# Nyström attention with a two-layer network: attention steps give way while TensorE's program block is on its way

## The chip, the cores and the metric

One core of one Trainium2 chip runs the kernel. The metric is device time of one execution in microseconds (us). The kernel before took 282.48 us, the median of three runs (282.12 to 282.77).

## The reference

Eight batches of eight heads, 576 positions, head dimension 64, all float32 in and out. Attention goes over 32 landmarks, each the mean of 18 neighbouring positions. Its output is the input of a normalised two-layer network with a residual.

```python
q_lm = q.reshape(B, H, m, S // m, D).mean(axis=3)      # m = 32
k_lm = k.reshape(B, H, m, S // m, D).mean(axis=3)
A  = sm(q, k_lm)                                       # sm: softmax of scaled products
Bm = sm(q_lm, k_lm)
C  = sm(q_lm, k)
Z = Bm.transpose(0, 1, 3, 2) / (norm1(Bm) * norminf(Bm) + 1e-06)
for _ in range(6):
    Z = 2 * Z - Z @ Bm @ Z
x = (A @ Z @ C @ v)                                    # then heads side by side: 8 x 576 x 512
xn = (x - mean(x)) / sqrt(var(x) + 1e-06) * g_ln
out = x + np.maximum(xn @ w_ch1, 0.0) @ w_ch2          # 512 -> 2048 -> 512
```

## The kernel before

All matmuls are fp16 with fp32 sums. Nothing in the kernel leaves the order of instructions to a scheduler: every instruction that `keep` records stays at its place in its engine's queue. The order is made while the program is built, by a planner inside the kernel.

**Four streams.** `run()` holds four generators. `attentions()` (number 0) makes the attention of the batches, in sets: batch 1, batch 2, batches 3 and 4, batches 5 and 6, batch 7 (batch 0 is done before `run()`). `first_layers()` (1) makes the hidden layer, batch by batch: 16 chunks of 128 hidden units, each four matmuls into a tile `psh`, then a relu into `hT`. `rows0[0]` (2) makes the attention rows of batch 0. `second_layers()` (3) makes the second layer from `hT` and `w2_16`, 16 matmuls with 512 columns for each block of 128 rows; batches 4 to 7 use seven products of half blocks instead of eight (the tiles `w2mix`).

**A step.** Each generator yields a function that says from which time on its next step could run without waiting, by the planner's own estimates. `run()` asks all four, takes the first in the order 0, 1, 2, 3 whose time has come, and lets it emit its instructions. So attention goes ahead of all else, and the second layer, which is always one matmul, fills what is left. If none is ready, the earliest is taken, or small matmuls on zeros (`warm`) are put in. `help_out()` gives VectorE, GpSimd and SyncE their side jobs in between: loads, casts (`nat`, `natv`), transposes (`xT`), landmark sums (`part`, `asum`), statistics, stores.

**The clock of the planner.** `Clock` keeps an estimate of when each engine is free and when each tile was written. It also counts matmuls. TensorE's program reaches the engine in blocks, and `Clock` assumes that a block holds `BLOCK` = 127 matmuls, that the first ends at matmul 116 (`mark`), and that the next one's fetch takes 5000 ns from the mark on while loads are running, 3300 ns otherwise (`fetched`). `calm(n)` returns `fetched` if n more matmuls would reach the mark, and 0 otherwise; once batch 3 is in its second layer (`late()`), 20 matmuls are added.

```python
def calm(self, n):

    return self.fetched if self.count + n + (20 if late() else 0) >= self.mark else 0.0
```

**Attention of a set** (`attention2`), in TensorE's order: landmark products and scores of the landmarks with k (`psec`), the gram product, then six iterations (`iterate`: 8 or 16 small matmuls into `bank`, then one update of `st` on VectorE), and between them, from `side_work`: the scores of q (`psea`), the product with v (`pscv`, 72 matmuls in two parts or one), and for each half batch `divisors`: two matmuls into `psd`, a logarithm and an exponential on ScalarE into `lns`, a product into `ea` on GpSimd. Then `pszt` and `pszc` (16 or 32 small matmuls), the copy `zt`, the products `zcbd` on VectorE, and at last the rows of the set (`rows_of`: two to four matmuls from `ea` and `zcbd` for each block of rows, then a copy into `xblk`). `psec`, `psea`, `pscv`, `psd`, `pszt`, `pszc` and the first layer's `psh` share two PSUM buffers; four banks serve the rest.

In the kernel before, `calm` is part of the time of three kinds of steps alone: the landmark and k scores (64 matmuls), the q scores (64), and the parts of the product with v.

**The first layer** of batch b+1 can begin when its attention is `ready` and the second layer is at batch b. Its `product_of_heads` makes 8 matmuls from `zt` and `w1_16` into two banks, which are cast to `m16`; `chunk` takes `m16` and `ea` to `psh`. While a first layer runs, the second layer can still do the batch before, as long as that has work left.

Of the kernel before, what the change touches and what calls it, by code (L numbers as in the profile page):

```python
# [20 lines left out]
def kernel(  # L21
# [196 lines left out]
    clock = Clock()  # L218
# [6 lines left out]
    class Ring:  # L225
# [16 lines left out]
        def next(self, tag, k=1):  # L242
            ring = self.rings.get(tag)
            if ring is None or len(ring) - 1 + k <= ring[0]:
                return 0.0
            olds = ring[1:len(ring) + k - ring[0]]
            if any(o in self.pinned for o in olds):
                return NEVER
            return clock.WAY + max(max(clock.wrote.get(o, (0.0,))[0], clock.used.get(o, (0.0,))[0])
                                   for o in olds)  # L250
# [215 lines left out]
    def warm(n, cols):  # L466
        idle = banks.take([P, 512])
        for _ in range(n):
            MM(idle[:, 0:cols], zeros[:, 0:P], zeros[:, 0:cols])
# [1014 lines left out]
    def attentions():  # L1484
        for c in sets:
            for y in range(len(c.units) // 2):
                yield lambda: c.spread_ready(y)
                c.spread(y)
            yield from attention2(c.bs, c)

    def first_layers():
        for b in range(B):
            yield lambda: 0.0 if b == 0 or (b in ready and current[0] == b - 1
                                            and (b <= LAST_WHOLE or len(centered) == 4)) else NEVER
            yield from first_layer(b)
            first_done.add(b)
            if b >= FAST:
                h_left.extend((b, i, k) for i in range(3) for k in (0, 4))
            if b == 0:
                keep_tail(0)  # L1500
# [3 lines left out]
    def second_layers():  # L1504
        for b in range(B):
            yield lambda: 0.0 if b in first_done else NEVER
            current[0] = b
            if b:
                keep_tail(b)
            yield from second_layer(b)  # L1510

    def run():
        streams = [attentions(), first_layers(), rows0[0], second_layers()]
        waits = [next(g) for g in streams]
        while any(waits):
            help_out()
            now = clock.now() + 60
            at = [w() if w else 2 * NEVER for w in waits]
            k = next((k for k in range(4) if at[k] <= now), None)
            if k is None:  # L1520
                k = at.index(min(at))
                if at[k] >= NEVER:
                    clock.free["PE"] = clock.now() + 200
                    stuck[0] += 1
                    assert stuck[0] < 2000, (at, current)
                    continue
                if at[k] > now + 250 and clock.share() < 0.5 and banks.next() <= now:
                    warm(1, 256)
                    continue
            waits[k] = next(streams[k], None)  # L1530
# [45 lines left out]
    next(a0)  # L1576
    next(a0)
    run()
    help_out(True)

# [29 lines left out]
```

## Time and profile before

| what | number |
|---|---|
| median of 3 runs | 282.48 us |
| the profiled execution | 282.81 us |
| its span, first to last instruction | 281.0 us |
| VectorE busy | 212.3 us (76%) |
| ScalarE busy | 161.9 us (58%) |
| mean granted TensorE clock | 0.997 |
| second layer, `bank<-w,hT`, 528 matmuls | 109.2 us busy |
| first layer, `psh<-ea,m`, 512 matmuls | 76.9 us busy |
| relu on ScalarE, `hT<-psh`, 115 | 71.0 us busy, 652 ns each |
| HBM read and written | 36.70 MB, 9.44 MB |

Times in a timeline are us from the span's start; a row is a run of like instructions, with start, length, engine, line, what is written and read, the count, and in brackets how long the engine stood idle before and what ended that. Matmuls overlap, so the length of one (0.38 us for a 512-column one) is more than its share of a run. All matmuls have the line of the helper that records them; they are told apart by their tiles. "issue" is a wait for nothing that the profile shows.

### The profile page before, as it was taken

The numbers are of one execution on the slowest core, as the hardware profiler recorded it, in microseconds if no ns is written. First come the engines' busy times: TensorE is split into PE (matmuls) and PEld (weight loads), VectorE is DVE, ScalarE is ACT, GpSimd is POOL, SyncE is SP. The second block draws the span as 40 slices with busy tenths as digits, with TensorE's granted clock in tenths as the row PEclk, the third lists the DMA queues.
The fourth block names the chain that finished last, engine by engine and source line by source line (L and its number), as shares of the span: only waits on it lengthen the run. The fifth ranks groups of instructions, "written<-read, shape, count | busy, mean of one in ns | idle before, by whom it ended". The sixth has DMA issues, their size and how long they took to land.

```text
span 281.0 us, 8678 instructions
## 1 busy us (share of the span) xinstructions
PE 266.2 (95%) x3618; PEld 165.6 (59%) x3618; DVE 212.3 (76%) x479; ACT 161.9 (58%) x287; POOL 160.1 (57%) x187
## 2 busy tenths in 40 slices
PE   7988999999999999889989999999999999999994
PEld 7744554355444564344555645567877666678883
DVE  3558985999999847888978384697885499748761
ACT  2676954368554887148889754698248733671000
POOL 5368778999999999978999999310000040100000
PEclk9999999999999999999999999999999999999998
DMA  7999999989745579893750101310060005300606
GB/s 244 384 387 388 388 388 392 354 278 266 246 126 160 152 249 304 265 279 95 221 188 2 34 8 45 72 40 0 2 144 9 1 5 118 72 0 2 149 22 167
DMA packets 23375, 46.70 MB, mean 166 GB/s; under 512 B 2212, under 2 KB 2472, under 8 KB 23336
## 3 DMA queue, kind: packets, MB, share of 16 engines
q1 hardware_dynamic: 23176, 46.02, 51.9%
q8 instruction: 28, 0.46, 0.7%
q10 hardware_dynamic: 160, 0.13, 0.2%
q14 instruction: 11, 0.09, 0.1%
HBM read 36.70 MB, written 9.44 MB: 164 GB/s over the span
## 4 chain that ended last, share of the span: by engine, by line
PE 79%; DVE 9%; ACT 5%; issue 3%; DMA 2%; SPq 0%; DVEq 0%; ACTq 0%
PE bank L274 51%; PE psh L274 21%; DMA stg<-in_q_dram 2%; ACT hT L268 2%; DVE xblk L268 2%; PE pscv L274 2%; DVE m L268 2%; DVE xT L268 1%; PE psec L274 1%; PE psd L274 1%; DVE part L268 1%; ACT ec L268 1%; DVE hT L268 1%; ACT lns L268 1%; PE psea L274 1%
## 5 line engine op out<-in xcount | busy, mean ns | idle before, releaser
L274 PE MATMUL bank<-w,hT 128*128 128x512 f16 (+1 forms) x528 | 109.2, 335 | 1.1 <-issue 1.0
L268 ACT ACTIVATE hT<-psh 128x576 f16<-128x576 f32 x115 | 71.0, 652 | 17.4 <-PE psh L274 16.0
L274 PE MATMUL psh<-ea,m 128*128 128x288 f16 x512 | 76.9, 286 | 2.8 <-ACT hT L268 2.1
L274 PEld LDWEIGHTS <-hT 128*128 128x128 f16 x656 | 60.4, 98 | 32.2 <-issue 6.9
L274 PEld LDWEIGHTS <-m 128*128 128x128 f16 x512 | 47.9, 97 | 25.3 <-issue 10.1
L268 DVE SCALAR_TENSOR_TENSOR xblk<-bank,rstd,xblk 128x256 f32<-128x256 f32 (+1 forms) x77 | 39.2, 541 | 18.2 <-PE bank L274 18.2
L268 POOL TENSOR_TENSOR ea<-ea,lns 128x576 f16<-128x576 f16 x14 | 18.1, 1306 | 47.2 <-ACT lns L268 47.0
L268 POOL CAST nat<-stg 128x1152 f16<-128x1152 f32 x28 | 32.6, 1181 | 2.0 <-DMA stg<-in_k_dram 1.1
L268 POOL CAST natv<-stg 64x1152 f16<-64x1152 f32 (+1 forms) x23 | 26.7, 1161 | 8.8 <-DMA stg<-in_v_dram 7.9
L268 ACT COPY xblk<-bank 128x512 f32<-128x512 f32 (+1 forms) x34 | 19.1, 588 | 12.2 <-PE bank L274 12.0
L268 DVE BATCH_NORM_STATS2 six<-xblk 128x6 f32<-128x512 f32 x36 | 24.2, 671 | 0.0
L268 ACT CAST m<-bank 128x512 f16<-128x512 f32 x30 | 17.0, 588 | 9.9 <-PE bank L274 9.9
L268 DVE STREAM_TRANSPOSE xT<-nat 128x576 uint32<-128x576 uint32 x28 | 21.4, 765 | 0.6 <-POOL nat L268 0.6
L268 ACT ACTIVATE lns<-psd 128x576 f32<-128x576 f32 x16 | 10.3, 646 | 17.8 <-PE psd L274 16.7
L268 DVE TENSOR_REDUCE part<-xT 128x32 f16<-128x576 f16 x28 | 20.0, 742 | 0.2
L268 POOL TENSOR_TENSOR asum<-asum 128x256 f32<-128x256 f32 (+1 forms) x28 | 18.0, 644 | 2.2
L268 DVE CAST m<-bank 128x512 f16<-128x512 f32 x18 | 12.2, 679 | 7.3 <-PE bank L274 7.2
L268 POOL TENSOR_TENSOR asum<-nat 128x512 f32<-128x512 f16 x14 | 16.5, 1178 | 1.1
L274 PE MATMUL bank<-w2mix,hT 128*128 128x256 f16 x128 | 16.5, 273 | 0.0
L274 PE MATMUL bank<-w2mix 128*128 128x256 f16 x128 | 16.0, 273 | 0.0
L268 DVE SCALAR_TENSOR_TENSOR st<-st,bank 128x128 f16<-128x128 f16 (+2 forms) x36 | 11.1, 308 | 6.4 <-PE bank L274 6.0
L274 PE MATMUL bank<-zcbd,ea 128*128 128x256 f16 (+1 forms) x80 | 14.4, 275 | 1.0 <-DVE m L268 0.8
(123 smaller groups left out, 341.6 us busy)
## 6 DMA issues: line engine op xcount, KB each, us to landing
stg<-in_q_dram SPq DMA_DIRECT2D x16, 576.0 KB, 5.7
stg<-in_k_dram SPq DMA_DIRECT2D x16, 576.0 KB, 5.4
stg<-in_v_dram SPq DMA_DIRECT2D x16, 576.0 KB, 7.1
out_dram<-xblk SPq DMA_DIRECT2D x70, 128.0 KB, 2.3
wstg<-in_moe_w_ch_dram SPq DMA_DIRECT2D x16, 512.0 KB, 7.1
out_dram<-xblk ACTq DMA_DIRECT2D x2, 64.0 KB, 2.3
out_dram<-xblk SPq DMA_DIRECT2D x2, 64.0 KB, 2.1
g_rows<-in_moe_g_ln_dram SPq DMA_DIRECT2D x1, 2.0 KB
```

What stands on the lines that cost most here:

```text
L268: return lambda *args, **kw: keep(getattr(self.engine, op)(*args, **kw))
L274: keep(nc.tensor.matmul(o, l, r, start=start, stop=stop, tile_position=(rb, cb), skip_group_check=(skip or cb != 0)))
```

## The change

The time of every step of stream 0 is raised to `calm(16)`. When 16 more matmuls (36 once batch 3 is in its second layer) would reach the planner's mark, no step of attention counts as ready before the estimated end of the fetch, whatever its own time was; the other streams' steps are taken in the meantime if they are ready. No instruction and no wait is put into the program by this line; only the order in which the planner emits steps, and what follows from it (which engine takes a copy, which side job comes when, how many warm matmuls are put in), can differ.

```diff
@@ -1516,6 +1516,8 @@
             help_out()
             now = clock.now() + 60
             at = [w() if w else 2 * NEVER for w in waits]
+            if waits[0]:
+                at[0] = max(at[0], clock.calm(16))
             k = next((k for k in range(4) if at[k] <= now), None)
             if k is None:
                 k = at.index(min(at))
```

## The prediction

> **What bounds the kernel.** I read the whole page first, then the chain of waits from 108 to 130 us, the stretches table, and last the timelines of TensorE and ScalarE from 119 to 147 us.
>
> ```profile
> span 281.0 us, 8678 instructions
> PE 266.2 (95%) x3618; PEld 165.6 (59%) x3618; DVE 212.3 (76%) x479; ACT 161.9 (58%) x287; POOL 160.1 (57%) x187
> q8 instruction: 28, 0.46, 0.7%
> ```
>
> TensorE sets the time: 266.2 of 281.0 us. Its program comes as 28 transfers of 16 KB. 0.46 MB over 7236 weight loads and matmuls is 64 bytes each, so one transfer holds 128 matmuls with their loads. Below, a matmul has its number in TensorE's order, from 0.
>
> ```profile
> 113.99 1.20 issue
> ...
> 119.25 0.49 issue
> ...
> 123.03 0.99 issue
> ```
>
> These three pieces of the chain are TensorE idle with nothing to wait for. They stand before matmuls 1503, 1631 and 1759, which are 128 apart: the ends of blocks. In the trace the transfers for them end at 113.58, 118.39 and 122.65, and the matmuls start 1.35 to 1.6 us later. Together 2.68 us; no other block end shows a gap of this kind. So 2.68 us is all that better timing of blocks can win.
>
> ```profile
> core 0: us, PE busy (x) PEld busy (x) DVE busy (x) ACT busy (x) POOL busy (x), PEclk, DMA share, GB/s
> 108.00:113.00 5.00, 5.00 (x120) 2.37 (x108) 4.82 (x14) 2.94 (x5) 4.68 (x7) 1.00 0.98 326
> 119.00:124.00 5.00, 3.54 (x130) 1.97 (x130) 3.93 (x12) 2.67 (x4) 4.68 (x6) 1.00 0.94 275
> ```
>
> Why there: the DMA engines are 0.98 and 0.94 busy, so the transfer for matmul 1503 starts only at 112.70, and the blocks are short of large matmuls. Matmuls 1631 to 1758 hold 72 of pscv and 47 of the iteration, but 5 of the second layer (0.216 us each: 11 of them from 172.36 to 174.73).
>
> [...]
>
> **The change, part by part.** It adds no instruction that waits. The planner only takes another stream's step while calm(16) says that the mark is near. By the two programs' orders attention stands back at five places: matmuls 612, 1631, 1754, 2374 and 2511. Added work: two warm matmuls (0.1 us each). Two relus and two casts of m16 go from ScalarE to VectorE, one row copy and one zt copy the other way.
>
> *Stalls at 1503 and 1631: kept.* The planner's marks are 116+127k (1513, 1640, 1767), the trace's ends 9, 9 and 8 matmuls sooner. Matmuls 1375 to 1502 hold 16 second-layer products in both programs, 1503 to 1630 hold 11 in both. So 1.20 and 0.49 stay: 0. Bounds -1.2 to +1.2, as loads that fall otherwise could free or delay a fetch.
>
> *Stall at 1759: removed.* At 1631 second-layer matmuls now stand first: the block holds 20 instead of 5. From rows: 119.74, 7 of them (1.51), 16 iteration products (0.22, 119.74 to 119.96), pscv (0.69), two psd (0.35), 2 second-layer (0.43), iteration 0.22, 2 (0.43), psd 0.35: 123.94. Matmul 1759 is the tenth of the next 12: 125.88, after the 124.02 at which its block was usable. Gain 0.99.
>
> *What pays for it: the chain to the next batch's first layer.* The 12 end at 126.53, the last iteration at 126.75; then both remaining psd pairs start (before: 125.31 for the last-but-one).
>
> ```profile
> 125.31 0.41 PE L274 MATMUL psd<-ea,bones 128*128 128x288 f16 x2
> 127.83 0.30 PE L274 MATMUL pszt<-st,cv 32*64 32x32 f16 x16
> 128.07 0.25 PE L274 MATMUL pszc<-cv,st 32*32 32x64 f16 x16
> 128.79 0.41 PE L274 MATMUL bank<-w,zt 64*32 64x512 f16 x8
> 130.88 0.65 PE L274 MATMUL psh<-ea,m 128*128 128x288 f16 x4
> 146.18 0.60 PE L274 MATMUL bank<-w,hT 128*128 128x512 f16 x2
> ```
>
> ```profile
> 125.81 0.65 ACT L268 ACTIVATE lns<-psd 128x576 f32<-128x576 f32 x1 [1.91 <-PE psd L274]
> 126.50 0.68 ACT L268 ACTIVATE lns<-lns 128x576 f32<-128x576 f32 x1
> 127.09 0.63 ACT L268 ACTIVATE lns<-psd 128x576 f32<-128x576 f32 x1
> 127.75 0.68 ACT L268 ACTIVATE lns<-lns 128x576 f32<-128x576 f32 x1
> 128.34 0.35 ACT L268 CAST zt<-pszt 128x256 f16<-128x256 f32 x1
> 129.26 1.07 ACT L268 CAST m<-bank 128x512 f16<-128x512 f32 x2 [0.57 <-PE bank L274]
> ```
>
> ScalarE works in order: the copy zt stands behind four passes over lns, so the eight products with zt start 3.48 us after the psd pair (125.31 to 128.79). Before, eleven second-layer matmuls (2.38), two psd pairs and 32 small products (0.42) filled these 3.48 us. Now only four (0.86), the pairs (0.59) and the 32 are left: 1.6 us of new idle time. 126.75+3.48 = 130.23 against 128.79: the chain is 1.44 late, with the gain of 0.99 already in it. Behind it the six second-layer matmuls that stood among the row products are used up too: 28 after 1631 before, 27 now, none after zt. TensorE has no filler until 146.18.
>
> How much of 1.44 lasts to 146.18 is settled by ScalarE, which paces the 16 chunks. From the start of zt (128.34) to the phase's last relu (ends 146.59) it spans 18.25 us, of which 2.30 idle (0.57, 0.21, 0.68, 0.19, 0.26, 0.20, 0.19 in its timeline): 15.95 of work. Changed: one relu fewer (0.60 pitch), one copy more (0.55): 15.9, from 126.75+3.03 = 129.78. With no idle it ends at 145.7 (0.9 early), with all of it at 148.0 (1.4 late). The first chunks now stand between the row products, so ScalarE has copies queued where it waited 0.21 and 0.68; the wait for m stays. That leaves about 1.5 idle: 147.2. Value +0.6, bounds -0.9 and +1.4.
>
> Cover that this needs: on POOL a nat cast with its sums (1.15+1.16+1.26+0.43 = 4.0) now stands ahead of the last two ea products. These end at about 133.35 instead of 129.8; the row products that read them come at about 134.9. Were that cover gone, they would be late by the difference, at most 1.
>
> *Place 612.* Before z, 20 second-layer matmuls instead of 18 from 600 on. The iterations queue behind two xblk updates on VectorE (1.41), so pszt starts at about 53.3 instead of 52.60, with 0.43 of work done ahead. The first chunk is then 1.0 late, since two reductions (1.34) stand ahead of the zcbd products. But VectorE, which is busy without a break from 53.06 to 62.32 and there ends the wait for m, has 9.26 us from zsum to the second m before and about 7.5 after (a transpose, three reductions and a row copy now stand ahead of it or on ScalarE, one w1 update of 0.87 comes in). From about 54.6 that is 62.1. 0, bounds -0.2 and +0.5. One k load goes ahead of stores in SP's queue, one pair of stores past another: SP stands idle on waits between them, 0.
>
> *Places 2374 and 2511.* TensorE has no idle gap over 0.2 us there and second-layer work remains until the first layer; the pairs of psd also stand together, but nine second-layer matmuls (1.94) cover the ScalarE chain. One iteration waits for its st behind cv on VectorE: +0.1, bounds -0.1 and +0.4. Place 1078, where only the order shifts: 0. From matmul 2900 on the orders agree.
>
> **Sum.** 0.6+0.1 = +0.7 us. Span 281.0 to 281.7. The profiled execution took 282.81 around its span; the median of the runs is 282.48, and 283.2 is against that. 0.2% (0.57 us) is what can be told from no change.
>
> **Rivals.**
> 1. *ScalarE absorbs it* (faster). If the 2.30 us of idle time give way as the chunks come earlier, the phase ends up to 0.9 sooner: about 281.6. For: so much idle time, fewer row copies in a lump. Against: it begins 1.44 later and psum buffers are two. Decides when over 1.44 of the idle time vanishes; under 281.9 when 1.9 does. Chance 0.19.
> 2. *The whole delay lasts*, or a fetch stall comes back elsewhere: 1.4 to 2.4 late, 283.9 to 284.9. For: no filler is left, and 1.60 us of idle are certain once ScalarE's order stands. Against: idle 0.89 falls away. 0.22.
> 3. *The change misses its aim and nothing shows*: gain and delay cancel, 282.5. Two of three stalls stay as the marks don't meet the trace's ends. 0.11.
>
> **Numbers.** Likeliest, partial recovery: 0.48, own range 282.8 to 283.9; of it 0.08 lies within 0.2%. So slower 0.40+0.22 = 0.62, same 0.08+0.11 = 0.19, faster 0.19. The range to leave about one in ten on either side: 281.5 to 284.5, which also takes in most of the fetch bound.
>
> **What would show it.** In the changed profile: issue gaps near 1.2 and 0.5 us before the psea products and in second-layer matmuls at 1631, none before 1759; TensorE idle some 1.6 us in all before and after pszc; zt some 3.4 us after the psd pairs; the second-layer matmuls after the run of 28 psh matmuls about 0.6 late. Wrong if the 1.20 gap is gone or doubled, or if zt isn't behind lns.

## The result, and the profile after

| | before | changed |
|---|---|---|
| median | 282.30 us (281.34 to 284.11, 6 executions) | 286.99 us (284.25 to 288.91, 6 executions) |
| ratio | 1 | 1.0118, interval 1.0071 to 1.0164 |
| the profiled execution | 282.81 us, span 281.0 us, mean clock 0.997 | 284.25 us, span 282.4 us, mean clock 1.000 |

The ratio and its interval leave out executions more than 1.5% above the fastest of their kernel (here 288.91), and they are not the quotient of the two medians, which is 1.0166.

The changed kernel is slower, and by more than the range allowed. The profiled execution of it is the fastest of the six: only 1.44 us above the profiled one before, where the medians lie 4.7 us apart. So there are two questions: where 1.4 us of the span went, and where the other executions lost 0.6 to 4.7 us more.

The head of the page of the changed kernel, span and busy times:

```profile
span 282.4 us, 8690 instructions
PE 265.4 (94%) x3620; PEld 166.7 (59%) x3620; DVE 217.2 (77%) x481; ACT 160.4 (57%) x285; POOL 160.2 (57%) x187
```

VectorE has two instructions more than before and 4.9 us more of busy time (217.2 against 212.3). That is too much for two casts (0.68 us each); some instructions must have become longer.

The stretches table of the changed kernel: busy time of each engine, granted clock (1.00 is full), share of the DMA engines, GB/s:

```profile
core 0: us, PE busy (x) PEld busy (x) DVE busy (x) ACT busy (x) POOL busy (x), PEclk, DMA share, GB/s
108.00:113.00 5.00, 5.00 (x128) 2.44 (x129) 4.67 (x13) 3.06 (x6) 4.68 (x7) 1.00 0.99 335
119.00:124.00 5.00, 5.00 (x125) 2.66 (x123) 4.90 (x13) 2.67 (x4) 4.68 (x7) 1.00 0.95 325
178.00:182.00 4.00, 1.39 (x8) 0.51 (x7) 4.00 (x7) 0.05 (x1) 1.72 (x2) 1.00 0.00 0
```

From 119 to 124 TensorE was busy for 3.54 of 5 us; now it is busy throughout. All three stalls at block ends are gone in this execution. The last row is new: from 178 to 182 TensorE works 1.39 us out of 4, where it was busy for all 4 before, and VectorE is busy the whole time.

TensorE's timeline of the changed kernel, first the stretch that the prediction spoke of, then the new gap:

```profile
124.89 0.67 PE L274 MATMUL psd<-ea,bones 128*128 128x288 f16 x4
125.40 1.03 PE L274 MATMUL bank<-w,hT 128*128 128x512 f16 x4
126.35 0.30 PE L274 MATMUL pszt<-st,cv 32*64 32x32 f16 x16
127.36 0.25 PE L274 MATMUL pszc<-cv,st 32*32 32x64 f16 x16 [0.71 <-ACT lns L268]
128.34 0.41 PE L274 MATMUL bank<-w,zt 64*32 64x512 f16 x8 [0.72 <-ACT zt L268]
...
145.17 0.61 PE L274 MATMUL bank<-w,hT 128*128 128x512 f16 x2
...
177.50 1.25 PE L274 MATMUL bank<-w,hT 128*128 128x512 f16 x5
181.31 0.93 PE L274 MATMUL bank<-zcbd,ea 128*64 128x256 f16 x4 [2.55 <-DVE zcbd L268]
```

The span divides at two points that both programs have. Matmul 1631 starts at 117.77 instead of 119.74: 1.97 earlier, 1.69 of it the two stalls (1.20 and 0.49) that are gone. From there to the second-layer matmuls after the first layer it takes 27.40 us (145.17 - 117.77) instead of 26.44: +0.96. From there to the end 137.2 instead of 134.8: +2.41. Sum -1.97 + 0.96 + 2.41 = +1.40, the difference of the spans. The +2.41 is the gap of 2.55 before the rows of batches 5 and 6. It ends on VectorE's `zcbd`.

First VectorE's and TensorE's rows of the kernel before at that place, then VectorE's timeline of the changed kernel around the gap, and GpSimd's:

```profile
177.96 1.41 DVE L268 TENSOR_TENSOR zcbd<-pszc,heads 128x256 f16<-128x256 f32 x4
...
179.94 0.68 DVE L268 TENSOR_TENSOR w2mix<-hT 128x1024 f16<-128x1024 f16 x1
```

```profile
177.68 1.47 PE L274 MATMUL bank<-w,hT 128*128 128x512 f16 x6
179.07 0.41 PE L274 MATMUL bank<-zcbd,ea 128*64 128x256 f16 x2
```

```profile
173.27 2.40 DVE L268 TENSOR_TENSOR w2mix<-hT 128x1024 f16<-128x1024 f16 x2
175.60 1.28 DVE L268 TENSOR_TENSOR w2mix<-w2mix,hT 128x1024 f16<-128x1024 f16 x2
176.81 3.46 DVE L268 TENSOR_TENSOR hT<-hT 128x1024 f16<-128x1024 f16 x2
180.19 0.74 DVE L268 SCALAR_TENSOR_TENSOR xblk<-bank,rstd,xblk 128x512 f32<-128x512 f32 x1
180.85 1.40 DVE L268 TENSOR_TENSOR zcbd<-pszc,heads 128x256 f16<-128x256 f32 x4
```

```profile
167.44 3.61 POOL L268 CAST natv<-stg 128x1152 f16<-128x1152 f32 x3
172.00 2.52 POOL L268 TENSOR_TENSOR ea<-ea,lns 128x576 f16<-128x576 f16 x2 [0.94 <-ACT lns L268]
176.51 3.21 POOL L268 TENSOR_TENSOR ea<-ea,lns 128x576 f16<-128x576 f16 x2 [1.98 <-PE bank L274]
```

Six mixings of half blocks (the side job that makes `w2mix` and the mixed `hT` for the second layer of the later batches) now stand ahead of the `xblk` update and of `zcbd`; before, they stood behind `zcbd`, and the row products followed the second layer with no gap. One of them takes 0.68 us. But the six took 1.80, 0.68, 0.68, 0.68, 1.77 and 1.76: the three long ones began while one of GpSimd's products into `ea` was running, and each ended 0.55 us after that product did. Three times 1.09 us is 3.3 us that six of 0.68 would not have taken.

TensorE had second-layer matmuls left (they follow the rows, from 182.07 on), but the row product stood ahead of them in its queue, and none of them ran in these 2.55 us.

### The profile page after: what moved, and what is told of

Read it like the earlier page. It is cut to its first block, busy times and chain, and to the rows that moved or that the text cites. A ratio compares the mean times of both kernels' runs of the same rounds, so it can differ in the third digit from the quotient of the medians.

```text
span 282.4 us, 8690 instructions
## 1 busy us (share of the span) xinstructions
PE 265.4 (94%) x3620; PEld 166.7 (59%) x3620; DVE 217.2 (77%) x481; ACT 160.4 (57%) x285; POOL 160.2 (57%) x187
## 5 line engine op out<-in xcount | busy, mean ns | idle before, releaser
L274 PE MATMUL bank<-w,hT 128*128 128x512 f16 (+1 forms) x528 | 107.7, 335 | 0.0
L268 ACT ACTIVATE hT<-psh 128x576 f16<-128x576 f32 x113 | 69.4, 651 | 19.3 <-PE psh L274 18.1
L274 PE MATMUL psh<-ea,m 128*128 128x288 f16 x512 | 75.9, 286 | 2.7 <-ACT hT L268 1.8
L268 POOL TENSOR_TENSOR ea<-ea,lns 128x576 f16<-128x576 f16 x14 | 18.7, 1352 | 46.9 <-ACT lns L268 44.8
L268 ACT CAST m<-bank 128x512 f16<-128x512 f32 x28 | 16.1, 590 | 8.5 <-PE bank L274 8.4
L268 DVE CAST m<-bank 128x512 f16<-128x512 f32 x20 | 13.6, 682 | 8.6 <-PE bank L274 8.6
L274 PE MATMUL bank<-w2mix 128*128 128x256 f16 x128 | 16.6, 273 | 0.0
L274 PE MATMUL bank<-w,zt 64*32 64x512 f16 x256 | 14.5, 386 | 1.7 <-ACT zt L268 0.7
```

What stands on the lines that cost most here:

```text
L268: return lambda *args, **kw: keep(getattr(self.engine, op)(*args, **kw))
L274: keep(nc.tensor.matmul(o, l, r, start=start, stop=stop, tile_position=(rb, cb), skip_group_check=(skip or cb != 0)))
```

## The experiments

Two theories stood at the start. **Mixings:** the 2.55 us gap comes from the six mixings ahead of `zcbd`; put behind it, they give the time back. **Late chain:** the delay at 127 to 131 us, which the prediction saw, costs the time, whatever happens later. A third came with the spread of the times: **clock**, that idle stretches lower TensorE's granted clock in most executions. The kernels below differ from the changed kernel or from the kernel before by the lines shown; the unused matmuls in some write to a free bank that nobody reads.

| kernel | starts from | median us (lowest to highest), executions | ratio to the kernel before | interval |
|---|---|---|---|---|
| mix_back | changed | 282.56 (281.64 to 284.45), 10 | 1.0004 | 0.9968 to 1.0041 |
| mix_first | before | 287.75 (285.47 to 289.52), 4 | 1.0151 | 1.0086 to 1.0216 |
| p_early | changed | 283.19 (282.39 to 285.40), 10 | 1.0023 | 0.9988 to 1.0058 |
| p_mid | changed | 282.21 (281.47 to 286.66), 10 | 0.9994 | 0.9961 to 1.0027 |
| p_late | changed | 282.98 (280.70 to 284.31), 10 | 0.9982 | 0.9941 to 1.0024 |
| warm_gap | changed | 286.73 (286.62 to 287.35), 4 | 1.0144 | 1.0102 to 1.0187 |
| after_again | changed | 286.29 (284.85 to 288.25), 12 | 1.0098 | 1.0063 to 1.0133 |
| warm_wide | changed | 285.69 (284.30 to 288.18), 12 | 1.0111 | 1.0071 to 1.0151 |
| after_third | changed | 286.70 (286.02 to 288.17), 6 | 1.0160 | 1.0128 to 1.0191 |
| warm_both | changed | 284.58 (284.27 to 285.23), 6 | 1.0079 | 1.0053 to 1.0106 |
| mix_back_fill | changed | 281.96 (281.33 to 282.25), 12 | 0.9971 | 0.9951 to 0.9991 |
| p_late_fill | changed | 283.73 (281.22 to 285.95), 12 | 1.0025 | 0.9983 to 1.0066 |

**The mixings put back (mix_back).** The hold stays everywhere; only the side job that mixes half blocks from `hT` (`mix_ahead`) may not be emitted between the last iteration and `zcbd` of batches 5 and 6.

```diff
@@ attention2
                 if it == 6:
                     banks.release(mine[0])
+                    no_mix[0] = bs == (5, 6)
...
+        no_mix[0] = False
         ready.update(bs)
@@ help_out
-            if (begun >= 0 and h_left and len(w2_mix) == 6 and clock.free["DVE"] <= now + 100
+            if (begun >= 0 and h_left and not no_mix[0] and len(w2_mix) == 6 and clock.free["DVE"] <= now + 100
```

> The changed kernel, but between the last iteration of the set of batches 5 and 6 and its zcbd products no half-block mixing (w2mix, hT) may be put on VectorE. Theory (the six mixings ahead of zcbd cost the time): TensorE's 2.55 us gap at 178.8 us falls under 0.3 us, the span goes from 282.4 to about 280, and the granted clock is 0.997 or more in every execution, so the median is about 281.8 us. Rival (the later first layer at 126 to 146 us costs the time): the gap goes but the time stays within 0.5 us of the changed kernel's profiled 284.2 us.

VectorE's timeline of mix_back, then TensorE's:

```profile
177.83 1.41 DVE L268 TENSOR_TENSOR zcbd<-pszc,heads 128x256 f16<-128x256 f32 x4
...
180.32 1.28 DVE L268 TENSOR_TENSOR w2mix<-hT 128x1024 f16<-128x1024 f16 x2
...
183.57 1.28 DVE L268 TENSOR_TENSOR hT<-hT 128x1024 f16<-128x1024 f16 x2
```

```profile
177.54 1.47 PE L274 MATMUL bank<-w,hT 128*128 128x512 f16 x6
178.94 0.73 PE L274 MATMUL bank<-zcbd,ea 128*64 128x256 f16 x4
```

`zcbd` is 3.0 us earlier (177.83 for 180.85), the row products follow the second layer with no gap, and each of the mixings shown takes 0.64 us (two in 1.28), since GpSimd's products no longer lie beside them. The time is that of the kernel before. The rest of the hold, with the late chain at 127 us in it, costs nothing in sum that can be measured. The theory missed in one part: it wanted a clock of 0.997 or more in every execution and about 281.8 us, and the clocks were 0.985 to 0.998. So something other than the gap at 178 us lowers the clock too.

**The mixings put first in the kernel before (mix_first).** No hold at all; after the sixth iteration of batches 5 and 6 the six mixings are emitted at once.

```diff
+                    if bs == (5, 6):
+                        while w2_left or len(w2_mix) < 6:
+                            mix_w2()
+                        while h_left and h_left[0][0] == 4:
+                            mix_ahead()
```

> The kernel before, without any hold, but with the six half-block mixings of batch 4 put on VectorE right after the last iteration of batches 5 and 6, ahead of zt and zcbd. Theory (their place alone makes the loss): TensorE idles 2 to 3.5 us before the first row product, single mixings take 1.2 us or more where GpSimd's ea products run beside them and 0.64 where not, and the time is 285 us or more. Rival (the loss needs the held steps): no gap over 1 us there, 282 to 283.5 us.

VectorE's, GpSimd's and TensorE's timelines of mix_first:

```profile
173.34 2.25 DVE L268 TENSOR_TENSOR w2mix<-hT 128x1024 f16<-128x1024 f16 x2
175.51 3.46 DVE L268 TENSOR_TENSOR w2mix<-w2mix,hT 128x1024 f16<-128x1024 f16 x2
178.89 3.45 DVE L268 TENSOR_TENSOR hT<-hT 128x1024 f16<-128x1024 f16 x2
...
183.25 1.40 DVE L268 TENSOR_TENSOR zcbd<-pszc,heads 128x256 f16<-128x256 f32 x4
```

```profile
175.12 6.67 POOL L268 TENSOR_TENSOR ea<-ea,lns 128x576 f16<-128x576 f16 x4
```

```profile
183.72 0.60 PE L274 MATMUL bank<-zcbd,ea 128*64 128x256 f16 x2 [2.91 <-DVE zcbd L268]
```

The order of the mixings alone makes a gap of 2.91 us and a kernel as slow as the changed one. All four `ea` products lie beside the mixings here. Five of the six mixings took 1.65 to 1.77 us; four of these lie beside an `ea` product, one beside GpSimd's last cast of `natv`. With mix_back the cause of the gap is shown from both sides. (Its profile also has the three stalls at block ends, 1.04, 1.05 and 1.54 us, so its time isn't the gap alone.)

**The hold at one place at a time (p_early, p_mid, p_late).** The added line is kept for marks in one third of the program.

```diff
-            if waits[0]:
+            if waits[0] and clock.mark < 1000:          # p_early
...
+            if waits[0] and 1000 < clock.mark < 2000:   # p_mid
...
+            if waits[0] and clock.mark > 2000:          # p_late
```

> The hold acts on the first of the five places only (the mark at matmul 624, about 47 us). Theory A (the order of loads and stores after it lets the fetch for matmul 1503 start sooner, as it did in the changed kernel, 111.2 instead of 112.7 us): the gaps of 1.20 and 0.49 us before matmuls 1503 and 1631 are gone, the one of 0.99 before 1759 stays or grows; 280.5 to 282.0 us. Theory B (that was chance of one execution): gaps as in the kernel before, 282.2 to 282.8 us.

> The hold acts on the second and third places only (marks 1640 and 1767, 117 to 124 us). Theory: the gap of 0.99 us before matmul 1759 is gone, the products with zt come about 1.4 us later, the second-layer matmuls after the run of psh come 0.6 to 0.7 us later, the mixings stand behind zcbd and no 2.55 us gap comes; 282.8 to 283.4 us, or 1 to 2 us less if the gaps before 1503 and 1631 are gone here too. Rival (the hold here is what costs the changed kernel its 4 us): 285 us or more.

> The hold acts on the marks after matmul 2000 only (the fourth and fifth places). Theory: since the mixings stand behind zcbd in this program, no gap over 0.5 us at 175 to 185 us and no difference from the kernel before beyond 0.4%: 282 to 283.5 us. Rival (holding back the steps there costs by itself): 284 us or more.

None of the three can be told from the kernel before by its interval, and none has the gap at 178 us: in each of the three programs the mixings stay behind `zcbd`. p_mid and p_late came out as their theories said. So no third of the hold makes the gap by itself; which of them it takes together was not tried. p_early's profile has none of the three stalls, though its hold acts only near 47 us, and its 283.19 us lies above the ranges of both its theories. p_mid holds the whole of what the prediction priced at +0.6 and comes out at 0.9994. In its profile the idle pieces at 127 to 131 us are there (0.49, 0.72 and 0.38), and the stalls before 1503, 1631 and 1759 are gone; how often the other executions of either kernel stall is not known. Up to matmul 1630 its order on TensorE is that of the kernel before, so the hold can't have removed the first two of these stalls.

**Small matmuls in the gap (warm_gap).** If the gap costs more than its length because the clock falls after it, matmuls on zeros there should give part back.

```diff
+        if bs == (5, 6):
+            gap_next[0] = 20
@@ rows_of
+                if gap_next[0]:
+                    warm(gap_next[0], 256)
+                    gap_next[0] = 0
```

> The changed kernel with 20 matmuls on zeros (256 columns, about 2.2 us) where TensorE stands idle for 2.55 us, before the first row product of batches 5 and 6. Theory (the gap lets the clock fall in some executions, which makes 284 to 289 us out of one program): every execution has a granted clock of 0.997 or more and 284.0 to 284.8 us. Rival (the clock falls for another reason, or differs by execution whatever the gap): clocks of 0.98 to 0.99 and times of 286 to 289 us come again.

This run is confounded. The planner counts `warm`, so later steps moved too, and new gaps of 0.72 and 0.97 us came before the matmuls at 233.01 and 243.24. Three of its four clocks were 1.00, but the times were 286.6 to 287.4, not the 284.0 to 284.8 of the theory. It decides nothing about the clock.

**Matmuls that the planner does not count (warm_wide), beside the changed kernel again (after_again).**

```diff
+    def fill_gap(n):
+        i = next(i for i in banks.order if i not in banks.held)
+        for _ in range(n):
+            tc.keep_in_program_order(nc.tensor.matmul(
+                banks.tiles[i][:], ident16[:], w2_16[:, 0, :], start=True, stop=True,
+                tile_position=(0, 0), skip_group_check=False))
...
+        gap_next[0] = bs == (5, 6)
@@ rows_of
+                if gap_next[0]:
+                    gap_next[0] = False
+                    fill_gap(10)
```

> The changed kernel once more, on the chip and beside the executions of the kernel before that the next three share. Theory: 284 us where the granted clock is near 1, 286 to 289 us where it is 0.980 to 0.995; the second kind in more than half of the executions; ratio to before 1.010 to 1.016. Rival (the six executions so far were a bad draw): a median under 284.5 us and clocks like those of the kernel before.

> The changed kernel with ten matmuls of 512 columns (2.2 us, their result is not used) at the place of the 2.55 us gap, and not one other instruction moved on any engine. Theory (TensorE standing idle there is what lowers the clock afterwards): clocks of 0.996 or more in nearly all executions, 284.0 to 284.8 us, median 2 us or more under that of the changed kernel beside it. Rival (clock falls have other causes): clocks and median as of the changed kernel, within 0.5 us.

The changed kernel came out as its theory said (clocks of 0.982 to 1.000, median 286.29 us; the ratio of 1.0098 is just under the range). The theory of warm_wide missed. Filling that one gap hardly helped: mean clock 0.9929 against 0.9923, median 0.6 us lower. But in warm_wide's profile the clock was lowered at 131.46, behind the idle pieces at 128 to 131 us, and once near the start (22.24, after a stall of 0.59 us at a block end). So the stretch at 128 us had to be filled as well.

**Both stretches filled (warm_both), beside the changed kernel a third time (after_third).** To warm_wide come three unused matmuls after `pszt` and three after `pszc` of batches 3 and 4:

```diff
+        if bs == (3, 4):
+            fill_gap(3)
         zsum = asm.tile([P, 2, W // 2], FP32, name="zsum", tag="zsum")
```

> The changed kernel with unused 512-column matmuls in both idle stretches of TensorE: ten in the one of 2.55 us, three before pszc and three before the products with zt of batches 3 and 4 (0.65 us each, at about 127 to 130 us). No instruction else is moved. Theory (the clock falls for 3.41 us after stretches in which TensorE is little used, and the changed kernel has two more of these): granted clock 0.996 or more in most executions, mean over 0.995, median about 284.5 us, 1 us or more under the changed kernel beside it. Rival (the clock is a matter of the chip): mean clock as of the changed kernel, within 0.001.

> The changed kernel on the chip of the other two, for its granted clock. Theory: mean clock 0.990 to 0.993, median 286 to 287 us. Rival (clock is a matter of the chip): mean clock within 0.001 of that of the kernel before.

after_third had a mean clock of 0.9908, as its theory said. Its stretches table, then that of warm_both:

```profile
core 0: us, PE busy (x) PEld busy (x) DVE busy (x) ACT busy (x) POOL busy (x), PEclk, DMA share, GB/s
127.00:131.00 4.00, 2.19 (x47) 0.99 (x45) 3.97 (x10) 3.41 (x7) 3.69 (x6) 0.92 0.67 200
131.00:134.00 3.00, 3.00 (x22) 1.75 (x20) 1.34 (x4) 2.12 (x5) 3.00 (x3) 0.54 0.22 57
178.00:184.00 6.00, 3.39 (x46) 1.39 (x44) 6.00 (x8) 2.16 (x4) 3.20 (x2) 1.00 0.10 22
184.00:189.00 5.00, 5.00 (x23) 2.80 (x23) 3.69 (x10) 2.77 (x5) 0.19 (x1) 0.66 0.23 52
```

```profile
127.00:131.00 4.00, 3.52 (x43) 1.78 (x41) 3.39 (x10) 3.39 (x7) 3.77 (x6) 1.00 0.72 213
131.00:134.00 3.00, 3.00 (x30) 2.07 (x28) 2.55 (x4) 2.89 (x7) 2.94 (x3) 1.00 0.00 0
...
182.00:187.00 5.00, 5.00 (x44) 3.34 (x43) 4.84 (x12) 4.12 (x9) 1.04 (x1) 1.00 0.23 52
```

In after_third each idle stretch is followed by one with the clock at 0.54 and 0.66: TensorE is "busy" all the time there and does 22 matmuls in 3 us where warm_both does 30. In warm_both the clock stays at 1.00, its six executions lie within 1 us (284.27 to 285.23, clock 0.997 to 1.000), and the median is 2.1 us below that of the changed kernel on the same chip. Nothing else was moved: every engine has its instructions in the same order in both, and neither profile has a stall at a block end. The clock is shown to be the second half of the loss.

**The mixings back and the mid stretch filled (mix_back_fill).** Both cures together: the lines of mix_back and the six unused matmuls of batches 3 and 4.

> The changed kernel with the mixings kept behind zcbd, and the six unused matmuls at 127 to 130 us. Theory: no stretch of low use is left between 60 and 270 us, so clock of 0.996 or more in most executions and 281.0 to 282.3 us, 0.3 to 0.6% under the kernel before. Rival: 282.5 us and clocks of 0.985 to 0.998 as without the six matmuls, no difference from the kernel before.

TensorE's timeline of mix_back_fill at 127 us; L475 is the unused matmul:

```profile
126.91 0.82 PE L475 MATMUL bank<-w,ident 128*128 128x512 f16 x3
127.68 0.25 PE L274 MATMUL pszc<-cv,st 32*32 32x64 f16 x16
127.87 0.82 PE L475 MATMUL bank<-w,ident 128*128 128x512 f16 x3
128.66 0.41 PE L274 MATMUL bank<-w,zt 64*32 64x512 f16 x8
```

The idle pieces are filled, and the products with `zt` start at 128.66 (128.39 without the filling). Twelve executions lie between 281.33 and 282.25, and the ratio of 0.9971 lies below 1 with its whole interval, if only just: on that chip this version is 0.7 us faster than the kernel before and 4.7 faster than the changed one. Against warm_both, which has the same clock (0.9986 and 0.9987 on average) and the mixings in front, it is 2.62 us faster: the price of the gap itself, 2.55 in the profile.

**The late hold alone, with a filling (p_late_fill).** Unused matmuls were put before `pszc` of batches 3 and 4 in p_late, to see whether the mid part of the hold is needed at all.

```diff
+        if bs == (3, 4):
+            fill_gap(4)
```

> The hold at the marks after matmul 2000 only, with four unused 512-column matmuls (0.87 us) before pszc of batches 3 and 4, where that program idles 0.91 us; nothing else is moved. Theory: clock 0.996 or more in most executions and 280.9 to 281.8 us, 0.4 to 0.7% under the kernel before. Rival: clocks of 0.992 to 0.994 in half of the executions as without the four, 282 to 283 us.

It gained nothing: 283.73 us where the theory had 280.9 to 281.8, with a clock of 0.996 or more in 7 of 12 executions. The filling closed the 0.91 us that p_late's profile had before `pszc`. But without the hold at 1631 the block before matmul 1759 is short again, and in the profile a stall of 2.08 us stands there, ahead of the filling: the fetch began 2.97 us after the block's first matmul, and a stretch of low clock follows (123.52 to 126.93). The run says little about the filling; from one profile, it suggests what the mid part of the hold is for.

## Why the prediction was wrong

**The failed step is "Places 2374 and 2511", put at +0.1 with bounds of -0.1 and +0.4.** From 145.17 to the end the profile shows +2.41, nearly all of it the one gap of 2.55 us. By themselves the two places behave as predicted (p_late, no gap): what failed is that they were priced place by place, on TensorE's work. The prediction looked whether TensorE has work left there, and found that it has. It did not ask in what order VectorE gets `zcbd` and the side jobs. The mixings are no step of attention and are not named in the diff, yet they moved past `zcbd`; and the 0.68 us of a mixing in the rows of the kernel before was measured without GpSimd's products beside it. Why they moved was not shown. By the planner's conditions the reason may be upstream: the casts of `natv` on GpSimd ended at 171.05 instead of 173.16, which would let the tiles for mixing come free sooner while VectorE looked free. mix_back has the early casts too (167.66 to 171.26) and no gap; so they alone cost nothing. The chain from the casts to the mixings was read from the conditions and not tried by itself.

**A term was missing: the clock.** No part of the sum priced what an idle stretch does to the granted clock. In the 24 executions of the changed kernel it was 0.999 or more in 3 (median 284.83 us), 0.993 to 0.994 in 13 (286.22), 0.987 to 0.988 in 4 (287.62) and 0.982 in 4 (288.31). One stretch of 3.41 us at half clock lowers the mean by 1.7/286 = 0.006; three of them cost 3.5 us by these medians, about 1.2 each. The kernel before loses some of this too: 5 of the 17 executions beside after_third had 0.993 or less. A mean of 0.996 to 0.998 need not be a loss: in the profiled execution before (0.997) the low clock begins at 279.15, after TensorE's last matmul has ended (276.86).

On one chip the medians step up like this: 282.69 before; mix_back_fill, that is the hold without its two faults, -0.73; the gap +2.62 (warm_both); the clock +2.12 (after_third): 286.70. They add up because each is the difference to the one ahead of it.

The profiled execution alone, 284.25 us, lies inside the predicted range. That is luck: 1.97 us gained ahead of matmul 1631, where the prediction had 0, stand against the 2.41, and its clock stayed at 1.00.

**"Stalls at 1503 and 1631: kept."** Wrong, and in a way that no order explains: they are gone here and in p_mid, whose order up to there is that of the kernel before. (The prediction itself had named the loss of the 1.20 gap as a sign of being wrong.) mix_first and p_late have the order of the kernel before on every engine up to 170 us: mix_first stalls for 1.04, 1.05 and 1.54 us, p_late not at all. The fetch of the next block began 4.67, 2.31 and 1.24 us after the block's first matmul in the profiled execution before, 3.01, 1.17 and 0.60 in the changed one, 0.60, 0.77 and 0.28 in mix_back, and 3.81, 1.56 and 2.97 in p_late_fill. They come and go between executions of one order. The prediction took one profile for a property of the program; only its bounds (up to -1.2) covered part of this. (Its marks lie 10, 9 and 8 matmuls behind the trace's block ends, not 9, 9 and 8; nothing rests on that.)

**"Stall at 1759: removed."** Right. In nine profiles with the hold at 1631, none has a stall there. Without it there were 0.99 (before), 1.54 (mix_first), 2.08 (p_late_fill), and none in p_early and p_late. With the hold the block takes about 6.15 us instead of 3.1 to 3.4, and fetches that began 2.12 (after_again) and 2.30 us (warm_gap) after its first matmul stalled nothing; without it, 1.24 did (before).

**"The chain to the next batch's first layer."** Right in mechanism and nearly in size. ScalarE's timeline of the changed kernel:

```profile
126.68 0.63 ACT L268 ACTIVATE lns<-psd 128x576 f32<-128x576 f32 x1
127.35 0.68 ACT L268 ACTIVATE lns<-lns 128x576 f32<-128x576 f32 x1
127.94 0.35 ACT L268 CAST zt<-pszt 128x256 f16<-128x256 f32 x1
```

`zt` stands behind the passes over `lns` as said, and the products with `zt` start 3.45 us after the `psd` pairs (predicted 3.48). TensorE idles 0.71 + 0.72 before and after `pszc` (predicted 1.6 us in all). From matmul 1631 to the second-layer matmuls after the first layer it is +0.96 instead of +0.6, within its bounds.

**"Place 612."** Put at 0, and about right: matmul 1375, behind it, starts at 108.18 instead of 108.04. The rest of the 1.97 us is in the next two blocks, which are shorter by 1.49 and 0.62.

**The rivals.** The second (283.9 to 284.9, "a fetch stall comes back elsewhere") is nearest in time, though 2 us short of the median, but neither of its mechanisms is what happened. No rival had VectorE's side jobs in it.

**Open.** Where exactly the kernel before loses clock in part of its executions, what delays a fetch, and how much idle time in one step of 3.41 us is enough to lower the clock were not settled. Which places of the hold together move the mixings was not settled either. Whether p_mid with a filling does as well as mix_back_fill was not tried.

## What to carry to other kernels

When a change lets a planner emit steps in another order, compare the order on every engine around every wait that ends on that engine, side jobs too: here six mixings that nobody waited for yet stood ahead of `zcbd`, and TensorE idled for 2.55 us. Price an idle stretch of TensorE at its length plus the lower clock that may follow (here 2.62 us for the gap and 2.12 for the clock, by the medians), and look at the spread of the times and the granted clocks before believing one profile. A stall that belongs to the timing of a transfer needs more than one profiled execution before it counts as a property of the program: in one order of instructions up to 170 us, mix_first stalled for 1.04, 1.05 and 1.54 us and p_late not at all.

## What the runs showed of the hardware

- **Low clock came in stretches of 3.41 us, after less idle time than that.** The stretches at half clock inside the program lasted 3.41 us each, and their edges lie on a grid of that step (full-clock stretches of 51.20, 98.99, 122.88 and 273.07 us are 15, 29, 36 and 80 steps; the last is in the profiled execution before). Idle pieces of 0.71 and 0.73 (after_third, before the low clock at 130.34) and one gap of 2.55 (before that at 184.96) were followed by a low stretch. What counted seems to be how much of one step of the grid was idle: the 2.55 of the profiled changed execution fell 1.22 and 1.33 into two steps, and the clock stayed at 1.00. But the idle share is not all of it. Between 60 us and TensorE's last matmul, low stretches followed steps in which no matmul ran for 1.50 to 2.06 us; none followed steps with 1.39 to 1.48 us, nor one with 1.76 (after_again, from 182.19).
- **VectorE's mixings took 2.6 times as long beside GpSimd's products:** 0.68 us alone, 1.76 to 1.80 beside them in the changed kernel, while one pair of GpSimd's went from 2.52 to 3.21 (the other pair kept its 2.52). Which began first told them apart in these rows: the three slowed mixings there, and the five in mix_first, began while a GpSimd instruction was running and ended 0.54 to 0.55 us after it; the one that began before GpSimd's (176.20, against 176.51) kept its 0.68.
- **A block of program was not always fetched in time:** over the 14 profiles, the fetch began 0.17 to 4.67 us after the block's first matmul for the same three block ends. In the kernel before and the changed one the DMA engines were 0.94 to 0.99 busy around the first and the third. Another block end, matmul 351 at about 22 us, stalled for 0.31 to 1.28 us in five of the profiles (after_again, p_early, p_mid, p_late, warm_wide) and for 0.24 or less in the others.
